# Softmax convolution and a squared-ReLU feed-forward: weight maxima and scaling on GpSimd, scaled chunks from chunk 4, closing sums next to each other

## The chip, the cores and the metric

The kernel runs on one core of one Trainium2 chip. The metric is the device time of one execution in microseconds. The kernel before takes 2104.97 us (median of 3 runs, 2104.33 to 2106.85). The engines are TensorE (PE, its weight loads PEld), VectorE (DVE), ScalarE (ACT), GpSimd (POOL) and SyncE (SP, which only issues transfers).

## The reference

A causal convolution of 7 taps whose weights come from a softmax for each position and head, and then a feed-forward block without a gate, all in float32.

```python
# x (8, 4096, 192), weight_gen (8, 4096, 8, 7), w_in (192, 2048), w_out (2048, 192)
w = weight_gen - np.max(weight_gen, axis=-1, keepdims=True)
w = np.exp(w)
w = w / (np.sum(w, axis=-1, keepdims=True) + 1e-09)
x_pad = np.concatenate([zeros((B, K - 1, D)), x], axis=1)
x_unf = x_pad[:, idx, :].reshape(B, S, K, H, D // H)     # idx: position + tap
x = np.einsum('bshk,bskhg->bshg', w, x_unf).reshape(B * S, D)
h = x @ w_in
r = np.maximum(h, 0.0)
out = (r * r) @ w_out
```

The inputs of the feed-forward weights arrive as float64 and are rounded to float32 in the kernel.

## The kernel before, in words

The 32768 positions are split over 128 partitions with 256 rows each, and worked through in 64 chunks of 4 rows a partition (512 positions). Chunks come in pairs (a group) that share one load of `x` and of the softmax logits. Float32 products are made of parts: each operand is a high part, rounded to the format TensorE takes, and a low part, the rest; high x high, high x low and low x high are added.

A chunk passes through these stages.

- Convolution (`conv_steps`, lines 326 to 500), two chunks ahead. VectorE: maximum (L353), subtraction (L354); ScalarE: exponential (L355); VectorE: sum, reciprocal, product (L356 to L358), then seven products with the taps (L384) and their adds (L397). Some adds are done by a transfer that accumulates (`moved`, L402), issued on GpSimd's queue. Then a transpose (L487) and transfers through DRAM (L493, L498) give `xT`; ScalarE makes the high part `xh` (L427) and VectorE the low part `xl` (L430).
- First product (`mm1`, L522), 8 steps j of a chunk, each 18 matmuls of 64 rows for two of the 16 blocks of the inner dimension.
- ScalarE: ReLU (L539), square (L546), high part (`high`, L550). VectorE: low part (`low`, L559 or L562), one step later.
- Second product (`mm2_turned`), two steps behind the first (LAG). Its 5 x 2 matmuls a block are L638 in an unscaled chunk. In a scaled chunk (`is_scaled`, chunks FIRST = 6 to 62) they are L603, L607 and L613; there the low parts are float16, so the softmax denominators and the weights are multiplied by powers of two that keep them in range, and 32 small matmuls (L613) stand at the end of the chunk in step 1 of the next one.
- Closing (`sum_turned`): ScalarE copies an accumulator (L648), VectorE adds its partner (L650), once for part 0 and once for part 1; only then may TensorE write these accumulators for the next chunk. Part 1 of a scaled chunk is also added across partitions by a transfer on GpSimd's queue (L652). Then transposes (L666, L670), transfers, and the scale of the output taken back (L689).

The weights are decoded during chunk 0 and 1: W holds the high and low parts of `w_in`, V those of `w_out`. For the scaled chunks the kernel needs the largest magnitude of each: `peak_v` (L294) and `peak_w` (L288), four VectorE reductions each in chunks 2 and 3, `spread_peaks` (L302) in chunk 3, step 4, which writes a pair of numbers for each partition to DRAM and reads all of them back on every partition (`dm`, then `tops`, a part of `du`), both on SP, and `coefficients` (L309 to L319) in chunk 3, step 7. `scale_v` multiplies V in place (L323, VectorE) and makes a float16 copy of its high part (L324, ScalarE), eight times, in chunk 5 from step 4 on and chunk 6. `measure` (L270) and `power` (L274 to L277) find a power of two for x, group by group.

Every engine works through its instructions in the order in which they are written. That order is written out by hand: `at(c, j, f)` puts a piece of work into step j of chunk c, `plan_conv` spreads the convolution's steps by a table (two steps of one convolution's end and two of the next one's softmax fall on step 1 of a chunk), and the loop from L878 on walks through the steps. In the step where a scaled chunk closes, the loop does the first two planned pieces (N_AHEAD), then `sum_turned` of part 0, then the other planned pieces, then the high parts, then `sum_turned` of part 1. `stage`, the pool of the tiles called `raw`, has three buffers, used by the weight loads and then by the closing sums.

Of the kernel before, what the change touches and what calls it, by code (L numbers as in the profile page):

```python
# [8 lines left out]
F32 = mybir.dt.float32  # L9
# [13 lines left out]
X_MIN = 2.0 ** -125  # L23
W_MIN = 2.0 ** -80
SHIFT = 2.0 ** 64
G_ROOT = 2.0 ** 8
V_ROOT = 2.0 ** 7
# [3 lines left out]
def kernel(  # L31
# [37 lines left out]
    NBUF = NF // 2  # L69
    FIRST = 6  # L70
    GL_POOL = 5
    SCALE_STEP = NJ
    N_AHEAD = 2
# [50 lines left out]
    scrap = du_flat[:, NF * D // 2 + N:].bitcast(BF16)  # L124
    peaks = const.tile([P, 8], F32, name="peaks")
    tops = du_flat[:, NF * D // 2:NF * D // 2 + 2 * P].bitcast(F32)
# [159 lines left out]

    def peak_w(k):
        nc.vector.tensor_reduce(  # L288
            out=peaks[:, k:k + 1], in_=W[:, 0, 2 * k:2 * k + 2, :].rearrange("p j w -> p (j w)").bitcast(F32),
            axis=AX.X, op=ALU.max, apply_absolute_value=True,  # L290
        )

    def peak_v(k):
        nc.vector.tensor_reduce(  # L294
            out=peaks[:, 4 + k:5 + k], in_=V[:, 4 * k:4 * k + 4, 0:D].bitcast(F32),
            axis=AX.XY, op=ALU.max, apply_absolute_value=True,
        )

    def spread_peaks():
        dm = dram.tile([P, 2], F32, name="dm")  # L300
        pk = coef[:, 4:6]
        nc.vector.tensor_reduce(out=pk, in_=peaks.rearrange("p (w k) -> p w k", w=2), axis=AX.X, op=ALU.max)  # L302
        nc.sync.dma_start(out=dm, in_=pk)
        nc.sync.dma_start(out=tops, in_=dm.rearrange("p w -> (p w)").rearrange("(o n) -> o n", o=1).broadcast_to([P, 2 * P]))

    def coefficients():
# [3 lines left out]
        nc.vector.tensor_scalar_max(top, top, W_MIN)  # L310
        w, v = top[:, 0:1], top[:, 1:2]
        ts(out=w.bitcast(U32), in0=w.bitcast(U32), scalar1=POW2, scalar2=None, op0=ALU.bitwise_and)
        ts(out=w_mul, in0=w, scalar1=SHIFT / G_ROOT, scalar2=None, op0=ALU.mult)
        ts(out=v.bitcast(U32), in0=v.bitcast(U32), scalar1=POW4, scalar2=1, op0=ALU.bitwise_and, op1=ALU.logical_shift_right)
        ts(out=v_unroot, in0=v, scalar1=SHIFT / V_ROOT, scalar2=None, op0=ALU.mult)
# [5 lines left out]
    def scale_v(j):  # L321
        v = V[:, 2 * j:2 * j + 2]
        nc.vector.tensor_scalar(out=v, in0=v.bitcast(F32), scalar1=v_mul, scalar2=None, op0=ALU.mult)  # L323
        nc.scalar.copy(V16[:, 2 * j:2 * j + 2], v[:, :, 0:D].bitcast(F32))  # L324

# [532 lines left out]

    for k in range(4):
        at(2, k + 3, lambda k=k: peak_v(k))  # L860
        at(3, k, lambda k=k: peak_w(k))
    at(3, 4, spread_peaks)
    at(3, 7, coefficients)
    for j in range(NJ):
# [10 lines left out]
    for u in range(1, NU):  # L875
        at(1, 2 * u, lambda u=u: dec(NU + u, 5))

    for c in range(1, NCH):  # L878
        tail = c == NCH - 1
        for j in range(NJ):  # L880
# [28 lines left out]
            if split_sum:  # L909
                for f in fs[:N_AHEAD]:  # L910
                    f()
                del fs[:N_AHEAD]
                sum_turned(done, (0,))
            elif done is not None:
                sum_turned(done)
            for f in fs:
                f()
            if c > 1:
                for part in range(2):
                    if j == (LOAD_STEP if tail else 2 * part + 2 if is_scaled(c - 1) else OUT_STEP + part):  # L920
                        store_turned(c - 1, part)
            if not tail or j < NJ // 2:
                for fb in fbs:
                    high(c, fb)
                    late.append(lambda c=c, fb=fb: low(c, fb))
            if split_sum:
                sum_turned(done, (1,))
            if c == 1 and j == 0:
# [61 lines left out]
```

## Time and profile before

| | |
|---|---|
| median of 3 runs | 2104.97 us |
| the profiled execution's own time | 2101.76 us |
| its span on the core | 2100.0 us |
| TensorE busy | 2074.4 us (99%) |
| VectorE busy | 1870.8 us (89%) |
| ScalarE busy | 1845.2 us (88%) |
| GpSimd busy | 221.2 us (11%) |
| chain that ended last | PE 71%, DVE 15%, DMA 6%, ACT 4% |

The durations in the rows further down come from that one execution. Busy time of TensorE is modelled and does not mean full speed; the weight loads' start times mark the steps more sharply, since 18 loads of L522 begin each step.

### The profile page before, as it was taken

What the parts mean: (1) busy time and instruction counts of PE and PEld (TensorE: products, weight loads), DVE (VectorE), ACT (ScalarE), POOL (GpSimd) and SP (SyncE); (2) the same over time, 40 slices, a digit from 0 to 9 for tenths busy, and PEclk for the clock granted to TensorE, in tenths of its full rate; (3) what the DMA queues carried; (4) which work ended last, traced back from release to release, by engine and by line L of the source; (5) the groups of instructions that cost most, each with busy time, mean ns of one, the idle gap of its engine ahead of it and who ended that gap; (6) DMA issues with size and microseconds to landing.
All of it is one profiled execution on the core that took longest, in us unless ns stands there. A gap on an engine that the chain in (4) does not pass through costs nothing.

```text
span 2100.0 us, 49532 instructions
## 1 busy us (share of the span) xinstructions
PE 2074.4 (99%) x19484; PEld 1707.0 (81%) x19484; DVE 1870.8 (89%) x2953; ACT 1845.2 (88%) x3551; POOL 221.2 (11%) x364
## 2 busy tenths in 40 slices
PE   9999999999999999999999999999999999999999
PEld 8887878878888788888888788787788878888878
DVE  9989899898898898998988988989889889999885
ACT  8887988889888899889898888998888988988986
POOL 0000110111110111101111101111011110011110
PEclk9999999999999999999999999999999999999999
DMA  9524454534545445445355354354453553544522
GB/s 234 101 51 98 108 117 97 122 73 105 125 97 110 93 91 118 113 98 121 70 110 126 94 113 93 90 120 106 104 120 71 110 125 93 116 85 97 122 59 56
DMA packets 322289, 217.78 MB, mean 104 GB/s; under 512 B 215696, under 2 KB 273168, under 8 KB 318216
## 3 DMA queue, kind: packets, MB, share of 16 engines
q1 hardware_dynamic: 300568, 181.17, 37.3%
q0 software_dynamic: 21488, 33.46, 9.4%
q8 instruction: 152, 2.49, 0.5%
q14 instruction: 81, 0.66, 0.1%
HBM read 106.52 MB, written 49.55 MB: 74 GB/s over the span
## 4 chain that ended last, share of the span: by engine, by line
PE 71%; DVE 15%; DMA 6%; ACT 4%; issue 2%; SPq 1%; DVEq 0%; ACTq 0%
PE ph L522 38%; PE acc L603 21%; DMA xT<-xd 4%; PE acc L607 4%; PE acc L613 4%; DVE pr L384 4%; DVE du L559 3%; DVE pr L397 3%; PE acc L638 3%; DVE xl L430 2%; DVE raw L650 1%; DVE gl L559 1%; ACT rg L539 1%; PE acc L570 1%; ACT rg L546 1%
## 5 line engine op out<-in xcount | busy, mean ns | idle before, releaser
L522 PE MATMUL ph<-xh,W 64*128 64x512 f32 x6096 | 1069.0, 403 | 0.0
L522 PEld LDWEIGHTS ph<-xh,W 64*128 64x128 f32 x6096 | 718.3, 186 | 100.9 <-ACT gh L550 23.0
L603 PE MATMUL acc<-gh,V 64*128 64x512 f32 x5472 | 772.9, 378 | 10.1 <-DVE raw L650 8.4
L539 ACT ACTIVATE rg<-ph 128x512 f32<-128x512 f32 x992 | 539.0, 596 | 197.8 <-PE ph L522 193.1
L603 PEld LDWEIGHTS acc<-gh,V 64*128 64x128 f32 x5472 | 594.4, 186 | 104.1 <-DVE raw L650 32.2
L546 ACT ACTIVATE rg<-rg 128x512 f32<-128x512 f32 x1007 | 580.5, 634 | 0.2
L550 ACT CAST gh<-rg 128x512 fp32r<-128x512 f32 x1008 | 576.1, 626 | 3.0 <-PE acc L580 3.0
L522 PE MATMUL ph<-xl,W 64*128 64x512 f32 x3048 | 495.3, 376 | 0.1
L559 DVE TENSOR_TENSOR gl<-rg,gh 128x512 f16<-128x512 f32 x570 | 389.6, 740 | 47.4 <-ACT gh L550 47.4
L384 DVE TENSOR_TENSOR pr<-xt,wt 128x768 f32<-128x768 f32 x440 | 412.3, 949 | 2.3
L522 PEld LDWEIGHTS ph<-xl,W 64*128 64x128 f32 x3048 | 361.5, 186 | 40.4 <-ACT xl L441 0.5
L397 DVE TENSOR_TENSOR pr<-pr 128x768 f32<-128x768 f32 x309 | 295.2, 955 | 6.1
L559 DVE TENSOR_TENSOR du<-rg,gh 128x512 f16<-128x512 f32 x342 | 232.0, 732 | 3.7 <-ACT gh L550 3.7
L607 PE MATMUL acc<-gl,du 64*128 64x512 f16 x1140 | 230.8, 381 | 1.0 <-DVE gl L559 1.0
L430 DVE TENSOR_TENSOR xl<-xT,xh 128x512 fp32r<-128x512 f32 x186 | 122.2, 687 | 122.0 <-ACT xh L427 121.8
L652 POOL DMA_DIRECT2D raw<-raw x57 | 47.3, 830 | 1261.3 <-DVE raw L650 1170.6
L607 PEld LDWEIGHTS <-du 64*128 64x128 f16 x1824 | 101.7, 95 | 62.3 <-issue 4.7
L607 PE MATMUL acc<-du 64*128 64x512 f16 x684 | 138.2, 382 | 0.0
L285 POOL DMA_DIRECT2D x_out<-x_fac x232 | 112.3, 493 | 42.5 <-DVE x_fac L282 41.4
L427 ACT CAST xh<-xT 128x512 fp32r<-128x512 f32 x186 | 108.1, 619 | 9.3 <-DMA xT<-xd 8.6
L402 POOL DMA_DIRECT2D pr<-pr x63 | 57.0, 905 | 531.3 <-DVE pr L384 484.8
L613 PEld LDWEIGHTS <-du 64*64 64x64 f16 x1824 | 48.3, 106 | 57.9 <-issue 24.1
(127 smaller groups left out, 1267.7 us busy)
## 6 DMA issues: line engine op xcount, KB each, us to landing
xT<-xd SPq DMA_DIRECT2D x124, 384.0 KB
xt<-in_x_dram SPq DMA_DIRECT2D x30, 1344.0 KB
out_dram<-o_sb SPq DMA_DIRECT2D x254, 96.0 KB
pr<-pr POOLq DMA_DIRECT2D x63, 384.0 KB, 5.8
xd<-xr SPq DMA_DIRECT2D x248, 96.0 KB
o_sb<-raw SPq DMA_DIRECT2D x342, 64.0 KB
raw<-raw POOLq DMA_DIRECT2D x57, 128.0 KB, 3.9
wt<-in_weight_gen_dram SPq DMA_DIRECT2D x31, 224.0 KB
```

The costliest lines, as they stand in the source:

```text
L285: nc.gpsimd.dma_start(out=fo[b * P // n:(b + 1) * P // n], in_=f[b::n])
L384: tt(out=dst, in0=src, in1=wf[:, t0 * H:t1 * H, k:k + 1].broadcast_to([P, m, G]), op=ALU.mult)
L397: tt(out=prs[k0], in0=prs[k0], in1=prs.pop(k), op=ALU.add)
L430: tt(out=parts["l"][:, k, n], in0=src[k][:, n], in1=parts["h"][:, k, n].bitcast(F32), op=ALU.subtract)
L522: nc.tensor.matmul(two[i], w, order(xx[rows, k]), start=(n == 0), stop=(n == last))
L539: nc.scalar.activation(r, ph, AF.Relu)
L546: nc.scalar.activation(r, r, AF.Square)
L550: nc.scalar.copy(gh, rgs[c, fb])
L559: nc.vector.tensor_tensor(out=gl, in0=g, in1=h, op=ALU.subtract)
L603: nc.tensor.matmul(acc[b + h], V[rows, fb, e:e + P], two_halves(g[rows]), start=fb == 0 and e < 2 * P, stop=False)
L607: nc.tensor.matmul(acc[h], V16[rows, 2 * j + i, 0:P], gls[c, j][rows, i], start=False, stop=last and i == 1)
L613: nc.tensor.matmul(acc[2 + h][i * D1:(i + 1) * D1], V16[rows, 2 * k + i, P:D], gls[c, k][rows, i], start=False, stop=k == NJ - 1, tile_pos ...
```

## The change

The sums of squares of a partition's weights take the place of the largest magnitudes; they are formed on GpSimd (`peaks_of`), folded down to 192 numbers a partition, and VectorE takes the maximum of these. They stand in chunk 1, step 0; the spread follows in chunk 1, step 7, with both transfers on GpSimd's queue, and the coefficients in chunk 2, step 2. V's scaling and its float16 copy are GpSimd's. FIRST is 4. In the closing step both closing sums come before the rest of the planned pieces.

```diff
-W_MIN = 2.0 ** -80
+W_MIN = 2.0 ** -123
-G_ROOT = 2.0 ** 8
+G_ROOT = 2.0 ** 9
...
-    FIRST = 6
+    FIRST = 4
     GL_POOL = 5
+    PEAKS = 192
...
-    def peak_w(k):
-        nc.vector.tensor_reduce(
-            out=peaks[:, k:k + 1], in_=W[:, 0, 2 * k:2 * k + 2, :].rearrange("p j w -> p (j w)").bitcast(F32),
-            axis=AX.X, op=ALU.max, apply_absolute_value=True,
-        )
-
-    def peak_v(k):
...
+    def peaks_of(pieces, k):
+        tt = nc.gpsimd.tensor_tensor
+        both = stage.tile([P, 2, NF * D // 4], F32, name="raw")
+        for i, w in enumerate(pieces):
+            o = both[:, min(i, 1)]
+            shaped = o if len(w.shape) == 2 else o.rearrange("p (a b) -> p a b", b=D)
+            tt(out=shaped, in0=w, in1=w, op=ALU.mult)
+            if i:
+                tt(out=both[:, 0], in0=both[:, 0], in1=o, op=ALU.add)
+        n, v = both.shape[2], both[:, 0]
+        while n > PEAKS:
+            n //= 2
+            tt(out=v[:, 0:n], in0=v[:, 0:n], in1=v[:, n:2 * n], op=ALU.add)
+        peaks[k] = v[:, 0:n]
 
     def spread_peaks():
         dm = dram.tile([P, 2], F32, name="dm")
         pk = coef[:, 4:6]
-        nc.vector.tensor_reduce(out=pk, in_=peaks.rearrange("p (w k) -> p w k", w=2), axis=AX.X, op=ALU.max)
-        nc.sync.dma_start(out=dm, in_=pk)
-        nc.sync.dma_start(out=tops, in_=dm.rearrange("p w -> (p w)").rearrange("(o n) -> o n", o=1).broadcast_to([P, 2 * P]))
+        for k in range(2):
+            nc.vector.tensor_reduce(out=pk[:, k:k + 1], in_=peaks[k], axis=AX.X, op=ALU.max)
+        nc.gpsimd.dma_start(out=dm, in_=pk)
+        nc.gpsimd.dma_start(out=tops, in_=dm.rearrange("p w -> (p w)").rearrange("(o n) -> o n", o=1).broadcast_to([P, 2 * P]))
 
     def coefficients():
...
-        w, v = top[:, 0:1], top[:, 1:2]
-        ts(out=w.bitcast(U32), in0=w.bitcast(U32), scalar1=POW2, scalar2=None, op0=ALU.bitwise_and)
+        tu = top.bitcast(U32)
+        ts(out=tu, in0=tu, scalar1=POW4, scalar2=1, op0=ALU.bitwise_and, op1=ALU.logical_shift_right)
+        ts(out=top, in0=top, scalar1=SHIFT, scalar2=None, op0=ALU.mult)
+        w, v, vu = top[:, 0:1], top[:, 1:2], tu[:, 1:2]
...
     def scale_v(j):
         v = V[:, 2 * j:2 * j + 2]
-        nc.vector.tensor_scalar(out=v, in0=v.bitcast(F32), scalar1=v_mul, scalar2=None, op0=ALU.mult)
-        nc.scalar.copy(V16[:, 2 * j:2 * j + 2], v[:, :, 0:D].bitcast(F32))
+        nc.gpsimd.tensor_scalar(out=v, in0=v.bitcast(F32), scalar1=v_mul, scalar2=None, op0=ALU.mult)
+        nc.gpsimd.tensor_copy(V16[:, 2 * j:2 * j + 2], v[:, :, 0:D].bitcast(F32))
...
-    for k in range(4):
-        at(2, k + 3, lambda k=k: peak_v(k))
-        at(3, k, lambda k=k: peak_w(k))
-    at(3, 4, spread_peaks)
-    at(3, 7, coefficients)
+    at(1, 0, lambda: peaks_of([W[:, 0, 2 * k:2 * k + 2].rearrange("p j w -> p (j w)").bitcast(F32) for k in range(4)], 0))
+    at(1, 0, lambda: peaks_of([V[:, 4 * k:4 * k + 4, 0:D].bitcast(F32) for k in range(4)], 1))
+    at(1, 7, spread_peaks)
+    at(2, 2, coefficients)
...
+    def highs_of(c, fbs):
+        for fb in fbs:
+            high(c, fb)
+            late.append(lambda fb=fb: low(c, fb))
...
+            if split_sum:
+                highs_of(c, fbs)
+                sum_turned(done, (1,))
             for f in fs:
                 f()
...
-            if not tail or j < NJ // 2:
-                for fb in fbs:
-                    high(c, fb)
-                    late.append(lambda c=c, fb=fb: low(c, fb))
-            if split_sum:
-                sum_turned(done, (1,))
+            if not split_sum and (not tail or j < NJ // 2):
+                highs_of(c, fbs)
```

Line numbers of the changed kernel are some 7 higher where the functions are the same. The first place is GpSimd's queue in chunk 1. Before, the accumulating transfers stand one behind the other; the third of the first row is chunk 2's tap 3, `pr<-prw` is its tap 4, and what follows belongs to chunks 3 to 5.

```order
L159 MEMSET xt 128x1152
L402 DMA pr<-pr 128x768
L402 DMA prx<-pr 128x768
L402 DMA pr<-pr 128x768 x3
L402 DMA pr<-prw 128x768
L402 DMA pr<-pr 128x768 x2
L402 DMA pr<-prw 128x768
L402 DMA pr<-pr 128x768 x2
```

In the changed kernel this is the end of the second sum of squares (on V) and what follows it on the same queue; the first sum, of the same make, stands ahead, directly behind the row `pr<-pr 128x768 x3`.

```order
L294 TENSOR_TENSOR raw<-V 128x768
L296 TENSOR_TENSOR raw<-raw 128x768
L300 TENSOR_TENSOR raw<-raw 128x384
L300 TENSOR_TENSOR raw<-raw 128x192
L409 DMA pr<-prw 128x768
L409 DMA pr<-pr 128x768 x2
L308 DMA dm<-coef 128x2
L309 DMA du<-dm 128x256
L409 DMA pr<-prw 128x768
L409 DMA pr<-pr 128x768
```

Chunk 2's tap 4 (the first `pr<-prw`) moved behind 18 GpSimd instructions, and chunk 3's (the second) behind the two transfers of the spread.

The second place is VectorE in the closing step of a scaled chunk, here chunk 23 closing in chunk 24 (the steps of the other scaled chunks read alike). Before:

```order
L384 TENSOR_TENSOR pr<-xt,wt 128x768
L397 TENSOR_TENSOR pr<-pr 128x768
L650 TENSOR_TENSOR raw<-acc_12036,raw 128x512
L353 TENSOR_REDUCE mx<-wt 128x32
L354 TENSOR_TENSOR wt<-wt,mx 128x224
L650 TENSOR_TENSOR raw<-acc_12038,raw 128x512
L559 TENSOR_TENSOR gl<-rg,gh 128x2x256 x2
```

And in the changed kernel:

```order
L391 TENSOR_TENSOR pr<-xt,wt 128x768
L404 TENSOR_TENSOR pr<-pr 128x768
L657 TENSOR_TENSOR raw<-acc_12008,raw 128x512
L657 TENSOR_TENSOR raw<-acc_12010,raw 128x512
L360 TENSOR_REDUCE mx<-wt 128x32
L361 TENSOR_TENSOR wt<-wt,mx 128x224
L566 TENSOR_TENSOR gl<-rg,gh 128x2x256 x2
```

The second closing sum moved ahead of the maximum and the subtraction; nothing else changed places.

The third place is VectorE from the spread to the coefficients, in chunks 1 and 2 of the changed kernel.

```order
L307 TENSOR_REDUCE coef<-raw 128x1 x2
L391 TENSOR_TENSOR prw<-xt,wt 128x768
L391 TENSOR_TENSOR pr<-xt,wt 128x768
L569 TENSOR_TENSOR gl<-rg,gh 128x512 x2
L391 TENSOR_TENSOR pr<-xt,wt 128x768
L404 TENSOR_TENSOR pr<-pr 128x768
L569 TENSOR_TENSOR gl<-rg,gh 128x512 x2
L657 TENSOR_TENSOR raw<-acc_826,raw 128x512
L657 TENSOR_TENSOR raw<-acc_824,raw 128x512
L404 TENSOR_TENSOR pr<-pr 128x768 x2
L360 TENSOR_REDUCE mx<-wt 128x32
L361 TENSOR_TENSOR wt<-wt,mx 128x224
```

Behind these rows stand two low parts and then the read of the maxima (`coef<-du`), which before stood in chunk 3, behind the low parts of its step 6.

## Rows read from the trace of the kernel before

**Rows 1.** The page, part 1: busy time of each engine.

```profile
PE 2074.4 (99%) x19484; PEld 1707.0 (81%) x19484; DVE 1870.8 (89%) x2953; ACT 1845.2 (88%) x3551; POOL 221.2 (11%) x364
```

**Rows 2.** Busy times by stretch: start:end, length, then busy time of each engine.

```profile
core 0: us, PE busy (x) PEld busy (x) DVE busy (x) ACT busy (x) POOL busy (x), PEclk, DMA share, GB/s
290.02:2025.58 1735.56, 1727.82 (x16419) 1406.39 (x16418) 1562.41 (x2431) 1545.00 (x2971) 197.51 (x323) 1.00 0.47 103
```

**Rows 3.** In order of time (start, length, what): weight loads, chunk 62.

```profile
2025.58 0.83 PEld L522 LDWEIGHTS ph<-xh,W 64*128 64x128 f32 x6
...
2035.32 0.51 PEld L522 LDWEIGHTS ph<-xh,W 64*128 64x128 f32 x6 [0.41 <-ACT gh L550]
...
2057.31 0.62 PEld L522 LDWEIGHTS ph<-xh,W 64*128 64x128 f32 x6
```

**Rows 4.** In order of time: ScalarE's copy and VectorE, chunk 29 closing.

```profile
1007.14 0.59 ACT L648 COPY raw<-acc 128x512 f32<-128x512 f32 x1 [0.16 <-PE acc L613]
...
1007.82 0.68 DVE L650 TENSOR_TENSOR raw<-acc,raw 128x512 f32<-128x512 f32 x1
...
1008.42 0.37 DVE L353 TENSOR_REDUCE mx<-wt 128x32 f32<-128x224 f32 x1
...
1008.83 0.39 DVE L354 TENSOR_TENSOR wt<-wt,mx 128x224 f32<-128x224 f32 x1
...
1009.14 0.68 DVE L650 TENSOR_TENSOR raw<-acc,raw 128x512 f32<-128x512 f32 x1
```

**Rows 5.** In order of time: weight loads of the same step.

```profile
1009.88 0.73 PEld L603 LDWEIGHTS acc<-gh,V 64*128 64x128 f32 x7 [0.39 <-DVE raw L650]
```

**Rows 6.** In order of time: SP, VectorE and TensorE around the coefficients, chunk 4.

```profile
137.63 12.19 SPq L680 DMA_DIRECT2D o_sb<-raw  x16
...
156.93 0.42 DVE L309 TENSOR_REDUCE coef<-du 128x2 f32<-128x256 f32 x1 [9.04 <-DMA du<-dm]
...
162.21 0.80 PE L638 MATMUL acc<-gl,V 64*128 64x512 f32 x2 [8.45 <-DVE gl L562]
```

**Rows 7.** Busy times by stretch: after TensorE's gap (columns as in rows 2).

```profile
162.20:166.20 4.00, 3.99 (x24) 3.32 (x26) 4.00 (x6) 0.92 (x2) 0.00 (x0) 0.64 0.94 334
```

**Rows 8.** In order of time: first weight loads of chunks 5, 6 and 8.

```profile
190.06 0.62 PEld L522 LDWEIGHTS ph<-xh,W 64*128 64x128 f32 x6
...
222.86 0.62 PEld L522 LDWEIGHTS ph<-xh,W 64*128 64x128 f32 x6
...
290.02 0.83 PEld L522 LDWEIGHTS ph<-xh,W 64*128 64x128 f32 x6
```

**Rows 9.** In order of time: VectorE and TensorE in chunk 1.

```profile
66.85 1.94 DVE L397 TENSOR_TENSOR pr<-pr 128x768 f32<-128x768 f32 x2
...
70.59 1.22 DVE L562 TENSOR_TENSOR gl<-rg,gh 128x512 fp32r<-128x512 f32 x2
...
70.56 0.59 PE L638 MATMUL acc<-gh,V 64*128 64x512 f32 x2
71.27 0.48 PE L638 MATMUL acc<-gl,V 64*128 64x512 f32 x2
```

**Rows 10.** Line L430 from 290 to 2030 us: VectorE's idle time before it.

```profile
  ACT xh L427: 113.9, 54
```

**Rows 11.** Groups by line: VectorE's maxima of W.

```profile
L288 DVE TENSOR_REDUCE peaks<-W 128x1 f32<-128x768 f32 x4 | 3.8, 943 | 0.0
```

**Rows 12.** In order of time: GpSimd in chunk 1.

```profile
57.72 0.86 POOL L402 DMA_DIRECT2D pr<-pr  x1 [1.11 <-issue]
60.19 0.86 POOL L402 DMA_DIRECT2D pr<-prw  x1 [1.62 <-DVE wt L354]
```

**Rows 13.** Groups by line (busy us, mean ns): GpSimd before 40 us.

```profile
L159 POOL MEMSET xt<- 128x1152 f32 x1 | 1.1, 1062 | 0.0
...
masks.py:199 POOL TENSOR_SCALAR_AFFINE_SELECT ident<-ident 128x128 f32<-128x128 f32 x1 | 0.3, 289 | 0.1
masks.py:197 POOL MEMSET ident<- 128x128 f32 x1 | 0.2, 205 | 0.0
```

**Rows 14.** Transfers by tile: KB each, median us from issue to landing.

```profile
pr<-prw POOLq DMA_DIRECT2D x2, 384.0 KB, 4.1
```

**Rows 15.** Busy times by stretch: chunk 1 (columns as in rows 2).

```profile
58.00:68.00 10.00, 10.00 (x96) 8.76 (x96) 9.11 (x15) 10.00 (x22) 1.43 (x2) 1.00 0.56 101
```

More of the change, by code (lines that the diff above doesn't have):

```diff
@@ L124 @@
     scrap = du_flat[:, NF * D // 2 + N:].bitcast(BF16)
-    peaks = const.tile([P, 8], F32, name="peaks")
+    peaks = {}
     tops = du_flat[:, NF * D // 2:NF * D // 2 + 2 * P].bitcast(F32)
@@ L285, in factor @@
             nc.gpsimd.dma_start(out=fo[b * P // n:(b + 1) * P // n], in_=f[b::n])
-    def peak_w(k):
-        nc.vector.tensor_reduce(
-            out=peaks[:, k:k + 1], in_=W[:, 0, 2 * k:2 * k + 2, :].rearrange("p j w -> p (j w)").bitcast(F32),
-            axis=AX.X, op=ALU.max, apply_absolute_value=True,
-        )
-    def peak_v(k):
[L294 to L297, printed above, removed]
+    def peaks_of(pieces, k):
[12 more added lines that the diff above has]
+        peaks[k] = v[:, 0:n]
     def spread_peaks():
@@ L310, in coefficients @@
         nc.vector.tensor_scalar_max(top, top, W_MIN)
-        w, v = top[:, 0:1], top[:, 1:2]
-        ts(out=w.bitcast(U32), in0=w.bitcast(U32), scalar1=POW2, scalar2=None, op0=ALU.bitwise_and)
+        tu = top.bitcast(U32)
+        ts(out=tu, in0=tu, scalar1=POW4, scalar2=1, op0=ALU.bitwise_and, op1=ALU.logical_shift_right)
+        ts(out=top, in0=top, scalar1=SHIFT, scalar2=None, op0=ALU.mult)
+        w, v, vu = top[:, 0:1], top[:, 1:2], tu[:, 1:2]
         ts(out=w_mul, in0=w, scalar1=SHIFT / G_ROOT, scalar2=None, op0=ALU.mult)
-        ts(out=v.bitcast(U32), in0=v.bitcast(U32), scalar1=POW4, scalar2=1, op0=ALU.bitwise_and, op1=ALU.logical_shift_right)
+        ts(out=vu, in0=vu, scalar1=POW4, scalar2=1, op0=ALU.bitwise_and, op1=ALU.logical_shift_right)
         ts(out=v_unroot, in0=v, scalar1=SHIFT / V_ROOT, scalar2=None, op0=ALU.mult)
```

## The prediction

> **What bounds the kernel now.** I read the page first. TensorE is busy for 99% of the span [rows 1], so time is gained or lost only where TensorE waits or takes more steps; the other engines count where TensorE waits for them. Then the busy times by stretch and the weight loads in order of time, which give the length of a chunk. From the 9th chunk (chunk 8, counted from 0) to the start of chunk 62, 54 chunks take 1735.56 us, 32.14 each [rows 2]. Chunk 62, whose step 1 carries no softmax steps, runs from 2025.58 to 2057.31, 31.73 us [rows 3]: the same matmuls without the wait. So a scaled chunk waits 0.41 us on average, 22.1 us over the 54.
>
> Where it waits is in the step after a chunk's last matmuls. As chunk 29 closes, ScalarE has copied the second accumulator by 1007.73, but VectorE runs first sum (1007.82), maximum (1008.42), subtraction (1008.83), and only then the second sum (1009.14, done 1009.82) [rows 4]. TensorE's weight loads for the next accumulation stop until 1009.88 [rows 5]. A load that stands idle is partly covered by matmuls still running, which is why I use chunk lengths, not these idle times.
>
> Three other places matter, all early. In chunk 4 VectorE waits 9.04 us for the broadcast maxima [rows 6], since the transfer that begins it stands on SP behind 16 stores from 137.63 to 149.82; the two transfers themselves end at 156.9, 7.1 us later. [...] Second, chunks 4 and 5 are unscaled; chunk 5 takes 32.80 us, from 190.06 to 222.86, and I count as much for chunk 4 without its wait. The first two scaled ones, chunks 6 and 7, take 67.16 together, to 290.02 [rows 8]. Third, in chunk 1 TensorE has no slack towards VectorE: its matmuls on a low part start at 71.27, 0.71 us after those before them at 70.56, on a low part begun at 70.59 [rows 9].
>
> **The change part by part.**
>
> *Closing sums.* With maximum and subtraction moved behind, the second sum starts about 0.62 us after the first (1008.42 less 1007.82 plus a hand-over), so it ends 0.7 us earlier, at about 1009.1 [rows 4], before the weights for that accumulator are wanted. Of the 22.1 us I keep 21: in a few chunks VectorE is so late that even the first sum comes too late, about 1 us in all. The softmax start is 0.7 us later, and the exponential runs in the step behind; VectorE waits 113.9 us in 54 places, 2.1 us a chunk, for ScalarE's high parts [rows 10], so there is room. Gain 21 us.
>
> *Coefficients.* The spread is now in chunk 1 and its two transfers are on GpSimd's queue. From there to the coefficients VectorE has some 11 us of other work; the transfers took 7.1. The wait goes: 8.45 + 1.4 = 9.9 us gained. The eight reductions (0.943 us for each of four on W [rows 11], and as many on V) go too, but stand beside a TensorE that had enough work; I count nothing for them. No wait stands behind them that would come out.
>
> *Two more scaled chunks.* If the scaled stretch begins without a wait, chunk 4 is two unscaled steps of 4.10 (32.80 / 8) and six scaled ones of 21.99 together (2035.32 to 2057.31 [rows 3]), 30.2, and chunks 5 to 7 take 31.73 each: 125.4 against 2 x 32.80 + 67.16 = 132.8, a gain of 7.4. If the first two scaled chunks wait as they do now (67.16 - 30.2 - 31.7 = 5.3), 2.1 is left. I take 4, since part of what they wait for, the copies on ScalarE and the scaling on VectorE, leaves these engines.
>
> *Sums of squares on GpSimd.* This is the loss. Eighteen instructions, 14 on 768 elements a partition, two on 384 and two on 192, stand in GpSimd's queue between the transfer issued at 57.72 and the one at 60.19 [rows 12]; that one, which adds tap 4 of chunk 2 to its sum, now waits for all eighteen. VectorE needs its result for the last add of chunk 2's convolution (the second of the two from 66.85 on, at 67.8 [rows 9]) and stands still in its queue until then; behind it are the transpose and the low part that TensorE has no slack for. The trace has no GpSimd instruction with two inputs. A one-input one took 289 ns for 128 elements, a memset 205 for 128 and 1062 for 1152 [rows 13]: the memset costs 0.84 ns an element on 0.10 us, and a read 0.66 ns more. One write and two reads come to 2.15 ns an element, 1.74 us for 768, 0.92 for 384, 0.51 for 192: 14 x 1.74 + 2 x 1.43 = 27.2 us. Bounds: the memset's rate (0.74 us, 11.7 in all) from below; a quarter more than my rate, 34 us, from above. With 27.2 the chain ends at 58.6 + 27.2 = 85.8, the transfer lands 4.1 us later [rows 14] at 89.9, and VectorE waits 22.1 us. TensorE waits as long, and pays the 1.4 us of clock seen in chunk 4: a loss of 23.5 us, from 8 to 30.
>
> [...]
>
> *Scaling and float16 copy on GpSimd.* Eight pairs, one to a step of about 4 us; at 1.50 ns an element a pair takes some 1.9 us, and the scaled weights are wanted six steps later. Nothing waits, if GpSimd does not hold up VectorE. *Coefficients, measuring and x's power two chunks earlier, and the move of chunk 3's tap 4 behind the spread's transfers:* 2.5 us of VectorE work in a chunk where low parts are a few tenths to 2 us ahead. I take 1.5, from 0 to 5.
>
> **Sum** against the profiled execution's own 2101.76: -21 - 9.9 - 4 + 23.5 + 1.5 = -9.9, 2091.9. The median of the runs is 2104.97, 3.2 above the profiled one; the forecast in those terms is 2095.
>
> **Rivals.**
>
> *VectorE and GpSimd hold each other up.* Then the eighteen run between VectorE's two-input instructions. VectorE is busy 9.11 of the 10 us from 58 on [rows 15], some 8.3 of it with two SBUF inputs, which end GpSimd's chain that much later; while it scales, GpSimd holds VectorE up by perhaps 1.5 of 1.9 us a step where VectorE has about 0.4 idle (1562.41 busy of 1735.56 [rows 2]), 9 at most in eight steps, 5 taken. 2095 + 8.3 + 5 = 2108, from 2102 to 2113. For it: VectorE is full and nearly all its instructions there have two inputs. Against it: no row; GpSimd does no arithmetic beside VectorE in this trace. It decides for slower once the mutual waiting is over 10 us. [...]
>
> *GpSimd is quick.* At the memset's rate the chain is over 15.5 us earlier: 2095 - 15.5 = 2080.
>
> *The closing sums give nothing back.* If VectorE, not the order of its instructions, set the chunk's length, the 0.41 us a chunk would return at the next low part: 2095 + 21 = 2116, slower. It decides where VectorE's idle time a chunk is under 0.41 us; it is 2.1 at one wait alone [rows 10], and chunk 62 ran freely with less VectorE work, so it is unlikely.
>
> **How the numbers follow.** The forecast 0.44 (its own range 2086 to 2102), mutual waiting 0.32, quick GpSimd 0.10, nothing from the closing sums 0.08, mixtures 0.06. What can be told from no change is about 0.2%, 4.2 us. Faster: 0.38 of the forecast (its upper end is within 4.2 us), 0.04 + 0.10 + 0.01 of the others, 0.53. Same: 0.06 + 0.17 + 0.02 = 0.25. Slower: 0.11 + 0.08 + 0.03 = 0.22. The range 2083 to 2112 takes in most of mutual waiting and leaves out the quick GpSimd and the last rival.
>
> **What would show it.** Closing sums: the two sums adjacent on VectorE, the weight loads of that step unbroken, chunks of 31.7 to 31.8 us. Coefficients: no wait of VectorE for the broadcast. Sums of squares: the eighteen on GpSimd at 1.74 us for 768 elements, the next transfer issued near 86, one VectorE wait of some 22 us at the last add of chunk 2, and a gap of TensorE as long in chunk 1 with a low clock behind it. Mutual waiting would show as longer VectorE adds or gaps between them beside GpSimd's, and a chain of 35 us. The prediction is wrong if TensorE shows no gap in chunk 1, or if the steady chunk stays at 32.1.

## The result, and the profile after

The changed kernel takes 2118.88 us (median of 4 runs, 2116.29 to 2122.32), the one before beside it 2104.65; the ratio is 1.0069, 95% interval 1.0051 to 1.0087. It is 0.7% slower, where I had forecast 2095 and a range up to 2112. Its profiled execution took 2119.23 us, the span 17.4 us more than before's 2100.0.

Lines of code stand 7 further down than before (L522 is L529, L562 is L569, L650 is L657). The page of the changed kernel, part 1 (compare [rows 1]):

```profile
span 2117.4 us, 49553 instructions
...
PE 2070.6 (98%) x19484; PEld 1693.2 (80%) x19484; DVE 1882.0 (89%) x2941; ACT 1837.1 (87%) x3545; POOL 289.2 (14%) x412
```

TensorE does the same work and is busy for less of a longer span. Where the span grew is read from the first weight load of each chunk:

| chunks | before, us | after, us | difference |
|---|---|---|---|
| 0 | 38.68 | 39.56 | +0.9 |
| 1 | 29.39 | 57.44 | +28.0 |
| 2 and 3 | 65.81 | 65.92 | +0.1 |
| 4 to 7 | 142.91 | 131.22 | -11.7 |
| 8 to 61 | 1735.56 | 1735.95 | +0.4 |

Chunk 1 is the loss. In order of time (start, length, what), GpSimd in chunk 1 of the changed kernel, answering to [rows 12]:

```profile
59.26 3.21 POOL L294 TENSOR_TENSOR raw<-W 128x768 f32<-128x768 f32 x2
62.55 2.41 POOL L296 TENSOR_TENSOR raw<-raw 128x768 f32<-128x768 f32 x1
...
86.17 1.47 POOL L294 TENSOR_TENSOR raw<-V 128x768 f32<-128x768 f32 x1
87.71 1.81 POOL L296 TENSOR_TENSOR raw<-raw 128x768 f32<-128x768 f32 x1
...
91.20 0.87 POOL L409 DMA_DIRECT2D pr<-prw  x1
```

The eighteen run from 59.26 to 91.2, 32 us, and the transfer of tap 4 leaves behind them, 31 us later than before. VectorE in the kernel before, where GpSimd has no such work:

```profile
58.31 0.95 DVE L384 TENSOR_TENSOR prw<-xt,wt 128x768 f32<-128x768 f32 x1
59.18 0.38 DVE L353 TENSOR_REDUCE mx<-wt 128x32 f32<-128x224 f32 x1
...
61.98 1.82 DVE L384 TENSOR_TENSOR pr<-xt,wt 128x768 f32<-128x768 f32 x2
```

And VectorE in the changed kernel:

```profile
59.29 4.00 DVE L391 TENSOR_TENSOR prw<-xt,wt 128x768 f32<-128x768 f32 x1
63.22 0.37 DVE L360 TENSOR_REDUCE mx<-wt 128x32 f32<-128x224 f32 x1
63.62 1.58 DVE L361 TENSOR_TENSOR wt<-wt,mx 128x224 f32<-128x224 f32 x1
65.13 4.17 DVE L569 TENSOR_TENSOR gl<-rg,gh 128x512 fp32r<-128x512 f32 x2
...
82.21 2.22 DVE L404 TENSOR_TENSOR pr<-pr 128x768 f32<-128x768 f32 x1
95.23 0.96 DVE L404 TENSOR_TENSOR pr<-pr 128x768 f32<-128x768 f32 x1 [10.81 <-DMA pr<-prw]
```

Two things are to be seen. The last add waits 10.81 us for the transfer, as forecast in kind. But the work ahead of it, from the multiplication at 59.29 to the end of the add at 84.4, takes 25.1 us; the same instructions took 9.5 before (58.31 to 67.8 [rows 9]). A multiplication takes 4.00 us instead of 0.95, the subtraction 1.58 instead of 0.39 [rows 4], while the maximum, with one input, keeps its time (0.37, 0.38 before). GpSimd's instructions are longer too: 2.41 us beside VectorE at 62.55, 1.81 for the same one at 87.71, where VectorE stands still. So 15.6 us of stretching and 10.8 of waiting reach TensorE, whose longest wait there is for a low part:

```profile
98.68 0.29 PEld L645 LDWEIGHTS acc<-gl,V 64*128 64x128 f32 x2 [12.38 <-DVE gl L569]
```

In the 3.30 us behind this wait the granted clock averages 0.56 (columns as in [rows 2]): the trace has it at 0.50 of full speed from 98.7 to 100.7 us and at 1.00 from 101.7 to 103.7. By an estimate, 3.30 x 0.44, that costs 1.5 us more:

```profile
98.70:102.00 3.30, 3.30 (x18) 2.68 (x20) 3.27 (x7) 0.00 (x0) 0.00 (x0) 0.56 0.42 86
```

Stretching, waiting and clock come to 27.9 us, near the 28.0 of the table. The wait for the broadcast maxima [rows 6] is gone; VectorE reads them in chunk 2 without idle time before it:

```profile
124.26 0.41 DVE L314 TENSOR_REDUCE coef<-du 128x2 f32<-128x256 f32 x1
```

The 54 steady chunks, chunks 8 to 61, did not move: 32.15 us each, which the prediction names as a sign that it is wrong. Busy times by stretch, as in [rows 2]:

```profile
307.28:2043.23 1735.95, 1721.32 (x16419) 1400.63 (x16418) 1560.97 (x2431) 1539.01 (x2971) 197.13 (x323) 1.00 0.47 103
```

That average hides two kinds of chunk. In order of time, a chunk in which the closing came as I forecast, from the stores of the transposed x (L500) and the loads of xT (L505) in chunk 20 to the closing in chunk 21:

```profile
707.85 1.81 SPq L500 DMA_DIRECT2D xd<-xr  x4
711.54 1.29 SPq L505 DMA_DIRECT2D xT<-xd  x2
...
717.76 0.62 ACT L434 CAST xh<-xT 128x512 fp32r<-128x512 f32 x1
...
734.86 1.28 DVE L657 TENSOR_TENSOR raw<-acc,raw 128x512 f32<-128x512 f32 x2
```

And two chunks later, from the transposition in chunk 22 on:

```profile
769.84 0.98 DVE L494 STREAM_TRANSPOSE xr<-pr 128x768 f32<-128x768 f32 x1
...
770.85 1.84 SPq L500 DMA_DIRECT2D xd<-xr  x4
776.10 1.29 SPq L505 DMA_DIRECT2D xT<-xd  x2
...
783.39 0.62 ACT L434 CAST xh<-xT 128x512 fp32r<-128x512 f32 x1 [2.37 <-DMA xT<-xd]
...
784.04 0.69 DVE L437 TENSOR_TENSOR xl<-xT,xh 128x512 fp32r<-128x512 f32 x1 [3.54 <-ACT xh L434]
...
800.50 1.28 DVE L657 TENSOR_TENSOR raw<-acc,raw 128x512 f32<-128x512 f32 x2
...
801.24 0.30 PEld L610 LDWEIGHTS acc<-gh,V 64*128 64x128 f32 x4 [1.88 <-DVE raw L657]
```

Both sums stand together in both (x2 in one row), so the edit does what it says. But in the second case the loads of xT leave 5.25 us behind the stores instead of 3.7, the high part starts 12.6 us behind the transposition's end instead of 9.9, VectorE waits 3.54 us for it, and the first sum comes 3.2 us into TensorE's step instead of 0.8. The chunk that follows, 23, takes 33.45 us, chunk 21 took 31.73. From the start of the low part to the end of the next transposition it is 20.6 to 20.8 us in every steady chunk of both kernels. So there is a loop beside TensorE's own pace: transposition, two transfers through DRAM, ScalarE's copy, VectorE's low part, 20.7 us of VectorE, transposition. A round of it is 31.2 to 33.8 us long after the change and 31.9 to 32.9 before; TensorE's shortest chunk is 31.52. The 2.1 us a chunk of [rows 10], which I took for room, is where this loop passes from the transfers to VectorE.

### The profile page after: what moved, and what is told of

Read it like the earlier page. It is cut to its first block, busy times and chain, and to the rows that moved or that the text cites. A ratio compares the mean times of both kernels' runs of the same rounds, so it can differ in the third digit from the quotient of the medians.

```text
span 2117.4 us, 49553 instructions
## 1 busy us (share of the span) xinstructions
PE 2070.6 (98%) x19484; PEld 1693.2 (80%) x19484; DVE 1882.0 (89%) x2941; ACT 1837.1 (87%) x3545; POOL 289.2 (14%) x412
## 4 chain that ended last, share of the span: by engine, by line
PE 67%; DVE 15%; DMA 6%; ACT 5%; issue 2%; POOL 1%; SPq 1%; DVEq 0%; ACTq 0%; POOLq 0%
PE ph L529 35%; PE acc L610 21%; DMA xT<-xd 6%; PE acc L614 5%; DVE pr L391 4%; PE acc L620 4%; DVE du L566 3%; DVE pr L404 3%; DVE xl L437 2%; PE acc L645 2%; ACT rg L546 1%; ACT gh L557 1%; DVE gl L566 1%; ACT rg L553 1%; ACT du L271 1%
## 5 line engine op out<-in xcount | busy, mean ns | idle before, releaser
L529 PE MATMUL ph<-xh,W 64*128 64x512 f32 x6096 | 1014.0, 404 | 0.0
L610 PE MATMUL acc<-gh,V 64*128 64x512 f32 x5664 | 761.9, 378 | 17.1 <-DVE raw L657 16.7
L529 PEld LDWEIGHTS ph<-xh,W 64*128 64x128 f32 x6096 | 674.7, 186 | 104.9 <-ACT gh L557 18.9
L529 PE MATMUL ph<-xl,W 64*128 64x512 f32 x3048 | 466.3, 376 | 0.1
L566 DVE TENSOR_TENSOR gl<-rg,gh 128x512 f16<-128x512 f32 x590 | 405.7, 744 | 22.0 <-ACT gh L557 21.6
L529 PEld LDWEIGHTS ph<-xl,W 64*128 64x128 f32 x3048 | 339.6, 186 | 36.2 <-ACT xl L448 0.5
L404 DVE TENSOR_TENSOR pr<-pr 128x768 f32<-128x768 f32 x307 | 296.0, 964 | 17.1 <-DMA pr<-prw 10.8
L566 DVE TENSOR_TENSOR du<-rg,gh 128x512 f16<-128x512 f32 x354 | 240.4, 733 | 3.7 <-ACT gh L557 3.7
L614 PE MATMUL acc<-gl,du 64*128 64x512 f16 x1180 | 216.9, 381 | 0.7 <-DVE gl L566 0.7
L614 PEld LDWEIGHTS <-du 64*128 64x128 f16 x1888 | 89.8, 95 | 81.1 <-issue 41.7
L614 PE MATMUL acc<-du 64*128 64x512 f16 x708 | 130.1, 382 | 0.0
```

The costliest lines, as they stand in the source:

```text
L404: tt(out=prs[k0], in0=prs[k0], in1=prs.pop(k), op=ALU.add)
L529: nc.tensor.matmul(two[i], w, order(xx[rows, k]), start=(n == 0), stop=(n == last))
L566: nc.vector.tensor_tensor(out=gl, in0=g, in1=h, op=ALU.subtract)
L610: nc.tensor.matmul(acc[b + h], V[rows, fb, e:e + P], two_halves(g[rows]), start=fb == 0 and e < 2 * P, stop=False)
L614: nc.tensor.matmul(acc[h], V16[rows, 2 * j + i, 0:P], gls[c, j][rows, i], start=False, stop=last and i == 1)
```

## The experiments

Each was compared with runs of the kernel before on the same chip; lengths of chunks are from its profile.

**e1 and e2: the closing sums alone, and all but the closing sums.** e1 is the kernel before with

```
+            if split_sum:
+                highs_of(c, fbs)
+                sum_turned(done, (1,))
             for f in fs:
...
-            if split_sum:
-                sum_turned(done, (1,))
```

and e2 the changed kernel with these lines taken back.

> The kernel before with only the closing sums moved ahead of the softmax steps. Loop theory (a steady chunk is set by the way from VectorE's transposition over the two transfers through DRAM, ScalarE's copy of the high part and VectorE's subtraction back to the next transposition, some 10 to 11 us of transfers and 20.7 us of VectorE without idle time): both sums come in time, but VectorE is no earlier at the next transposition, so the 54 chunks stay near 32.1 us; gain 0 to 10 us, 2095 to 2105. Rival 'real but given back' (the sums gain the 21 us that I forecast, and another part of the change spoils the steady chunks): 2084, chunks of 31.75. Rival 'the new order is itself harmful': over 2108.

> The changed kernel with the second closing sum put back behind the softmax steps and the high parts; all else as changed. Loop theory: the same time as the changed kernel within 5 us, 2114 to 2124. Rival 'real but given back': if the early parts of the change spoil the steady chunks by themselves, undoing the sums loses a further 21 us, about 2140.

e1: 2089.24 us, ratio 0.9942 (0.9930 to 0.9954). e2: 2124.35 us, ratio 1.0106 (1.0089 to 1.0122). The 54 chunks of e1, then of e2:

```profile
290.34:2014.14 1723.80, 1719.93 (x16420) 1393.82 (x16418) 1560.56 (x2431) 1540.83 (x2971) 197.75 (x323) 1.00 0.48 104
```

```profile
305.65:2049.49 1743.84, 1731.01 (x16420) 1406.83 (x16418) 1563.98 (x2431) 1544.02 (x2971) 197.70 (x323) 1.00 0.47 102
```

Neither theory had it whole. The sums are worth 11.8 us in the steady chunks on their own and 7.9 in the changed kernel, not 21 and not nothing. And the early parts, which touch no line of a steady chunk, cost 8.3 us there (e2 against [rows 2]). Four edits that I had priced one by one were not independent.

**e3: GpSimd's chain behind the transfer that it held up.**

```
-    at(1, 0, lambda: peaks_of(...))
...
-    at(1, 7, spread_peaks)
-    at(2, 2, coefficients)
+    at(2, 3, coefficients)
...
+    at(1, 1, lambda: peaks_of(...))
...
+    at(2, 0, spread_peaks)
```

Both calls of `peaks_of` stand behind `plan_conv` of chunks 2 and 3 here.

> The changed kernel with the 18 sums of squares queued on GpSimd behind the transfer of chunk 2's tap 4 instead of ahead of it (spread and coefficients one step later with them). Theory 'place in the queue': the stall of 28 us in chunk 1 falls to about 6 (now chunk 3's three transfers stand behind the chain), some 2097. Rival 'mutual hold-up': VectorE's longer instructions beside GpSimd's are what TensorE waits for, and 18 us or more of the stall stay, 2109 or more.

2109.62 us, ratio 1.0037 (1.0025 to 1.0049); chunk 1 takes 49.58 us, still 20.2 more than before. GpSimd and VectorE in chunk 1 of e3, in order of time:

```profile
60.88 0.86 POOL L409 DMA_DIRECT2D pr<-prw  x1 [1.61 <-DVE wt L361]
61.44 3.22 POOL L294 TENSOR_TENSOR raw<-W 128x768 f32<-128x768 f32 x2
...
61.46 5.98 DVE L569 TENSOR_TENSOR gl<-rg,gh 128x512 fp32r<-128x512 f32 x2 [0.79 <-ACT gh L557]
67.36 4.70 DVE L391 TENSOR_TENSOR pr<-xt,wt 128x768 f32<-128x768 f32 x2
72.10 2.10 DVE L404 TENSOR_TENSOR pr<-pr 128x768 f32<-128x768 f32 x1
74.12 3.42 DVE L241 TENSOR_TENSOR V<-du,V 128x512 fp32r<-128x512 f32 x2
...
95.51 1.28 DVE L569 TENSOR_TENSOR gl<-rg,gh 128x512 fp32r<-128x512 f32 x2
```

The transfer leaves first and VectorE never waits from 62 to 97 us, yet up to the chain's end at 94.7 most rows with two inputs take twice their usual time or more (4.70 for two multiplications that take 1.82 before). Behind it the two low parts are back at 1.28 us. The place in the queue was worth 8 us; the hold-up of two engines is the rest. My condition for the rival (2109 or more) is met.

**e4: the first split of x one step later** in the changed kernel, which takes the transfers out of the loop.

```
-                at(m - 1, NJ - 3 if k == 0 and is_scaled(m) else NJ - 2, f)
+                at(m - 1, NJ - 2, f)
```

> The changed kernel with the first split of a scaled chunk's x (ScalarE's high part, VectorE's low part) one step later, in the step of the second. VectorE's work is the same; only its wait for the transfers is taken out of the loop. Loop theory: steady chunks of 31.55 to 31.75 us, 54 x 0.5 = 27 us less, about 2092. Rival 'VectorE's work alone sets the length': chunks stay at 32.15, 2119 within 4. Rival 'given back by the early parts': no change either.

2102.89 us, ratio to before 1.0004 (0.9996 to 1.0013). The 54 chunks:

```profile
308.55:2029.59 1721.04, 1721.04 (x16420) 1404.14 (x16418) 1562.66 (x2432) 1540.75 (x2971) 197.69 (x323) 1.00 0.47 104
```

31.87 us each, and every chunk alike within 0.02. The loop theory's sign is right, since VectorE's work is the same 1562 us; its size is not (14.9 us of the 27 expected): VectorE, now later in its order, starts the first sum 1.4 us into the step in every chunk.

**e5 and e6: where TensorE's code stands.** What spoils some chunks repeats with a period of 8. So do the packets of TensorE's code, the transfers that bring its instructions; the transfer queues of the changed kernel (packets, MB, share):

```profile
q8 instruction: 152, 2.49, 0.5%
```

152 packets of 16 KB for 38,968 instructions of TensorE is one for 256.4. TensorE starts 4864 of them in 8 scaled chunks, and 19 packets begin there (114 in chunks 8 to 55, before and after), one for 256; that the packets are TensorE's code is my inference from these counts. By it they come at the same places every 8 chunks, and, by an estimate, moved by 32 instructions they hit the same places in other chunks (3 chunks are 1824 instructions, 7 x 256 and 32). After the change chunk 8 stands 9 instructions later in this code: between 186.6 and 214.0, in chunks 4 to 6, TensorE has nine semaphore instructions that it does not have before. I moved the code by tiny matmuls at the very start, 12 in the changed kernel (e5), 4 in the kernel before (e6):

```
+    for _ in range(12):
+        nc.tensor.matmul(awake[:, 0:16], ident, ident[:, 0:16], start=True, stop=True)
```

> The changed kernel with twelve tiny matmuls (16 columns, result unused) ahead of everything, so that TensorE's instructions stand 24 places later in its code. In the traces TensorE's code comes in packets of 16 KB, 19 of them in 8 chunks (4864 instructions), and one that begins within about 3 us behind the transposition ends the stores to DRAM 1 to 1.5 us late. The change moved TensorE's place in this rhythm by 9 instructions; with 24 more it stands as before (33, of a pattern that repeats every 32). Code-load theory: the 54 steady chunks fall from 1736 to some 1725, as with the closing sums alone, and the time from 2119 to some 2109. Rival 'another effect of the early parts' (GpSimd's transfers, the buffers' rotation): steady chunks stay within 3 us of 1736, 2119 to 2121.

> The mirror image: the kernel before with four tiny matmuls ahead of everything, 8 instructions, which puts TensorE's code where the changed kernel has it (9). Code-load theory: the 54 steady chunks rise from 1735.6 to some 1743, as in the changed kernel with the old sums, worst in the chunks of number 1, 2 and 7 modulo 8 instead of 4 and 5, and the time to some 2110. Rival 'another effect of the early parts': steady chunks within 3 us of 1735.6, worst in 4 and 5, 2102.

The expectations count two instructions for each tiny matmul. The pages, e5's and then e6's, show four, two matmuls and two weight loads (19484 of each without them):

```profile
PE 2070.5 (98%) x19508; PEld 1667.0 (79%) x19508; DVE 1881.6 (89%) x2941; ACT 1838.3 (87%) x3545; POOL 289.4 (14%) x412
```

```profile
PE 2079.6 (99%) x19492; PEld 1710.2 (81%) x19492; DVE 1871.5 (89%) x2953; ACT 1842.8 (87%) x3551; POOL 220.8 (10%) x364
```

So the code moved by 48 and 16 instructions, not by 24 and 8. Counted from the kernel before and in a repeat of 32, e6 stands at 16 where the changed kernel has 9, and e5 at 25 (9 + 48 - 32) where I meant it to stand at 1.

e5: 2109.41 us, ratio 1.0026 (1.0017 to 1.0035). e6: 2115.95 us, ratio 1.0056 (1.0044 to 1.0069). The 54 chunks of e5, then of e6:

```profile
309.10:2033.38 1724.28, 1717.37 (x16419) 1367.44 (x16418) 1560.17 (x2430) 1539.89 (x2970) 197.15 (x323) 1.00 0.47 104
```

```profile
290.88:2035.62 1744.74, 1729.94 (x16419) 1406.13 (x16417) 1563.14 (x2431) 1542.71 (x2971) 197.16 (x323) 1.00 0.47 102
```

One moved 11.7 us down, the other 9.2 us up; 1725 and 1743 were expected. As neither stood where it was meant to, it is partly luck that the sizes fit so well. What the two show is that unused instructions ahead of everything move the steady chunks by this much, in e6 with none of the early parts there. Mean length of the chunks 8 to 61 by number modulo 8:

```
              0      1      2      3      4      5      6      7
before      31.98  32.05  32.19  32.08  32.42  32.40  31.98  31.98
e6          31.98  32.69  32.15  32.18  32.01  32.02  31.98  33.59
e2          31.98  32.90  32.44  32.31  31.99  31.99  31.98  32.77
after       31.77  32.69  32.15  32.22  31.83  31.64  31.60  33.38
e5          31.73  31.62  31.62  32.18  32.18  31.73  31.71  32.77
```

Sixteen unused instructions give the kernel before nearly the pattern of the changed one, longest in 1 and 7. The 48 do not give back that of before: in e5 the chunks of number 7 stay the longest. The transfers' records show how the packets act.

Over before, after, e1, e2, e5, e6 and e11 (chunks 8 to 60, 371 in all), a code packet begins within 3.2 us behind the transposition in 100 chunks; the stores to DRAM then end 4.05 us behind it (median) and in 84 of the 100 later than 3.6. In the other 271 they end at 3.13, and 10 are later than 3.6.

A second place shows in the same records. Where no packet begins within 3.2 us but one does 5.5 to 8.3 us behind the transposition (30 chunks; the bounds are read off these rows), the stores end on time, at 3.16, but the high part, which waits for the loads of xT, starts at 11.59 us (median), in 25 of the 30 at 11 or later. In the 241 chunks with a packet in neither place it starts at 10.62, in 21 at 11 or later. The long chunks of number 1 in "after" and e6 follow such packets, those of number 7 the packets at the stores.

How late the high part starts gives the next chunk's length:

```
high part behind the transposition, us   chunks   next chunk, us
under 10                                    26        31.73
10 to 11                                   254        31.90
11 to 11.5                                  50        32.45
11.5 to 12                                  17        32.83
over 12                                     24        33.48
```

**e7 and e8: the kernel before with the late split and the spread's two transfers on GpSimd's queue**, with (e7) and without (e8) the closing sums' move.

> The kernel before (maxima on VectorE, scaled from chunk 6 on) with three edits: the closing sums moved ahead, the spread's two transfers on GpSimd's queue, and the first split of a scaled chunk one step later. Loop theory with what the runs gave: chunks of 31.87 as with the changed kernel's late split, 14.5 us less, and VectorE's wait for the maxima gone, 10 us less: about 2077. If the late split helped only because of the early parts' rhythm: chunks of 31.92 or more, 2080 to 2090.

> The same without the closing sums' move: the kernel before with the late split and the two transfers on GpSimd's queue. It shows what the closing sums are worth once the transposition is no longer late. If the sums' place is a bound of its own, as I forecast: chunks of 32.1 and 12 us or more slower than with the move, about 2090. If the loop alone set the chunks: the same as with the move within 4 us, about 2077.

e7: 2082.83 us, ratio 0.9899 (0.9885 to 0.9912). e8: 2120.71 us, ratio 1.0084 (1.0070 to 1.0098). Their 54 chunks, e7 first:

```profile
285.48:2006.17 1720.69, 1720.69 (x16420) 1403.56 (x16419) 1561.98 (x2432) 1540.60 (x2971) 196.81 (x323) 1.00 0.47 104
```

```profile
283.41:2043.19 1759.78, 1727.94 (x16420) 1403.52 (x16418) 1565.55 (x2432) 1543.23 (x2971) 196.82 (x323) 1.00 0.47 101
```

VectorE in chunk 18 of e8, where chunk 17 closes, in order of time:

```profile
620.40 0.68 DVE L650 TENSOR_TENSOR raw<-acc,raw 128x512 f32<-128x512 f32 x1
621.00 0.37 DVE L353 TENSOR_REDUCE mx<-wt 128x32 f32<-128x224 f32 x1
621.41 0.39 DVE L354 TENSOR_TENSOR wt<-wt,mx 128x224 f32<-128x224 f32 x1
621.72 0.68 DVE L650 TENSOR_TENSOR raw<-acc,raw 128x512 f32<-128x512 f32 x1
```

With the transfers out of the loop every chunk of either kernel is alike, and the sums' place is worth 39.1 us, where I expected 12 or more: 0.72 a chunk, as much as the maximum and the subtraction between the two sums take there (621.00 to 621.72). This is the mechanism that I had forecast, free of the loop. The late split without the sums' move makes the kernel slower, the sums alone gain 12.8 us; together, with the queue, they gain 21.

**e9 and e12: what the wait for the maxima had covered.** The steady chunks of e7 came out as expected, its time 6 us over the 2077, and its chunk 4 still takes 39.81 us. e9 puts the coefficients later; e12 also puts chunk 3's load of x earlier.

```
-    at(3, 7, coefficients)
+    at(4, 2, coefficients)
...
-            if j == (LOAD_STEP if c > 1 else 0) and c % 2 ...
+            if j == (2 if c == 3 else LOAD_STEP if c > 1 else 0) and c % 2 ...
```

> The kernel before with late split, closing sums ahead, the spread's transfers on GpSimd's queue, and now the coefficients three steps later (chunk 4, step 2). In the run without this last edit chunk 4 still took 39.8 us, because the second transfer stood behind its first on GpSimd until 143.8 and VectorE came for its result too early. If VectorE's wait for the maxima is all that chunk 4 loses: chunk 4 falls to about 33, 7 us less, 2076. Rival: the chunk waits for something else there as well (the kernel before with its wait took 42.9, one with the late split alone 36.6), and 3 us or more stay, 2079 or more.

> The run with the later coefficients, and in chunk 3 alone the load of the next x group three steps earlier, ahead of that chunk's 28 stores on SP instead of behind them. In the run before it ScalarE's measuring waited 6.2 us in chunk 4 for that load (and VectorE 3.5 us), which VectorE's wait for the maxima had covered in the kernel before. If that is what is left of chunk 4's loss: chunk 4 from 39.2 to some 33, 2077. Rival: a third wait stands behind it, or the early load takes the transfers' time from chunk 3: 2081 or more.

e9: 2083.31 us, ratio 0.9907 (0.9893 to 0.9920); chunk 4 still 39.16 us, so the rival's condition (2079 or more) is met. ScalarE in chunk 4 of e9:

```profile
167.03 1.48 ACT L270 ACTIVATE du<-xt 128x1536 bf16<-128x1536 f32 x1 [6.24 <-DMA xt<-in_x_dram]
```

In the kernel before ScalarE came to this instruction at 169.82 without a wait: VectorE's 9.04 us [rows 6] had covered it. e12: 2079.27 us, ratio 0.9892 (0.9876 to 0.9909), chunk 4 at 32.81 us, what an unscaled chunk takes [rows 8]. Of the 6.4 us the profiled run of e12 gave 2.2 back by a later start of chunk 0 (15.4 us against 13.2), which I can't explain; that start lies between 13.1 and 13.8 in the other profiles, but for e5's with its matmuls ahead (16.1). e12 beats both kernels.

**e10: both low parts another step later.**

```
-        splits = [split(k) for k in range(ND)]
+        splits = [lambda k=k: high_part(k) for k in range(ND)] + [lambda k=k: low_part(k) for k in range(ND)]
...
+                at(m - 1, NJ - 2 if k < ND else NJ - 1, f)
```

> The same, with both low parts of a scaled chunk's x another step later, behind both high parts: VectorE no longer waits 2.1 us a chunk for ScalarE's high part. If that wait is what makes the first closing sum 0.6 us late in every chunk (it starts 1.38 us into the step, its input is there at 0.69): chunks of 31.55 to 31.73, 8 to 16 us less than with the low parts in place. Rival 'the high part's place in ScalarE's order sets it, or the low parts come too late for the next chunk's first matmuls': no gain, or a loss of several us.

2132.97 us, ratio 1.0144 (1.0128 to 1.0159). A miss: step 2 falls to 3.58 us as hoped, but step 0 rises from 3.68 to 4.88, because the low parts come too late for the next chunk's first matmuls; 32.72 us a chunk.

**e11: w_out's scaling back on VectorE and ScalarE** in the changed kernel.

```
-        nc.gpsimd.tensor_scalar(out=v, ...)
-        nc.gpsimd.tensor_copy(V16[...], ...)
+        nc.vector.tensor_scalar(out=v, ...)
+        nc.scalar.copy(V16[...], ...)
```

> The changed kernel with w_out's scaling back on VectorE and its float16 copy back on ScalarE; all else as changed. Mutual hold-up: GpSimd's scaling of 2.2 to 3.7 us a pair stretches VectorE's low parts beside it from 1.28 to 1.9 us, in chunks 3 to 5; without it those chunks lose 1 to 4 us less, 2115 to 2118. Rival 'GpSimd takes the work off VectorE at no cost': VectorE has 0.8 us more a step and the chunks are 1 to 4 us longer, 2120 to 2123.

2106.47 us, ratio 1.0016 (1.0007 to 1.0025), 12 us under the changed kernel. Chunks 3 to 5 fell by 0.8 us, so the hold-up there is small. The gain is in the steady chunks, 1725.25 us, which this edit does not touch: a high part over 12 us behind the transposition comes in 2 chunks instead of 7. TensorE's code stands at the same place here, with the nine semaphore instructions. In chunk 30 the packet begins at 3.1 us behind the transposition and does no harm, where in the changed kernel it began at 2.8 and did. In the chunks of number 0 modulo 8 it begins 5.6 to 7.8 us behind the transposition in the changed kernel, and the next chunk takes 32.4 to 33.0 us; here it begins at 8.4 or later in five of seven, and 31.52 follows; in the other two it begins at 7.2 and 8.3, and 32.53 and 33.35 follow. That fits the code packets; what moved them against the transposition was not tried.

## Why the prediction was wrong

- **Closing sums, -21: the step that failed**, where the prediction says "Of the 22.1 us I keep 21". It took the first sum's time as given and only moved the second. The runs show that the first sum comes at the end of the loop over DRAM; where the high part is late, what the move spares TensorE is lost again. In the changed kernel's surroundings the move is worth 7.9 us (e2), alone 11.8 (e1), free of the loop 39.1 (e7, e8). The supporting reading, "so there is room", was wrong: the 2.1 us were a wait in that loop.
- **A missing term, +8.3.** The early parts slow the steady chunks (e2), and moving TensorE's code alone does so too (e6, 9.2 us by 16 instructions); the long chunks are those where a code packet falls on the stores or loads. The nine instructions of the change are not enough by themselves: e11 has them, and its steady chunks are only 1.5 us longer than e1's (1725.25, 1723.80). What else moves the packets against the transposition stays open. No term and no rival had any of this.
- **Sums of squares, +23.5: right in kind, 28.0 measured.** A 768-element instruction at 1.47 to 1.81 us where VectorE stands still is what I estimated (1.74). But the queue's wait was 10.8 us instead of 22.1, and 15.6 came from stretched VectorE instructions; the clock's 1.5 was right (1.4). e3 shows that mending the queue alone saves 8. The rival that had this mechanism gave it 13 us; alone it costs 20.
- **Coefficients, -9.9: right, 10.1** (chunk 4's 42.94 us against 32.81 for an unscaled one). The 8.45 is TensorE's wait in [rows 6]; no run shows the 1.4 by itself, it is an estimate from [rows 7], 4.00 us at a mean clock of 0.64 (4.00 x 0.36). In chunk 4 of the changed kernel the granted clock is 1.00. That nothing stands behind the wait was wrong for a kernel scaled from chunk 6 on (e9); the changed kernel escapes most of it (ScalarE waits 2.8 us for that load).
- **Two more scaled chunks, -4: 1.6** (132.8 us without the wait against 131.2). A pair of scaling and copy on GpSimd took 3.7 us on average instead of 1.9; e11 puts what that held up at 0.8 us.
- **The rest, +1.5: 0.1** in chunks 2 and 3, where it was expected. Chunk 0 is 0.9 longer, which no term covers; it lies between 38.67 and 40.94 us in the profiles.

The measured terms sum to -7.9 + 8.3 + 28.0 - 10.1 - 1.6 + 0.1 + 0.9 = 17.7, the span's difference is 17.4. The rival "the closing sums give nothing back" comes near in time (2116) but not in cause: VectorE's work does not set the chunk, since e4 and e7 shorten it with the same work.

## What to carry over

When an engine idles in every round and the same stretch of work follows each time, the idle time need not be room; follow it back to its own start, and if that closes a loop, compare the loop's length with the bound engine's. Price edits of one loop together, and after a wait is taken away look at what was waiting beside it. Here a GpSimd chain of two-input instructions next to a full VectorE cost VectorE's time (15.6 us of stretching in chunk 1), not only its own queue's (10.8).

## What I had not expected of the hardware

- Where a 16 KB packet of TensorE's code fell among the small stores to DRAM, they ended 0.9 us late (median 4.05 against 3.13 us, 100 and 271 chunks); where one fell on the loads behind them, the high part was about 1 us late (11.59 against 10.62, 30 and 241 chunks). Sixteen unused instructions at the start cost 9.2 us in 54 chunks of one kernel, 48 gained 11.7 in the other.
- Beside GpSimd's two-input instructions VectorE's with two inputs took as much as four times as long (0.95 to 4.00 us), a reduction with one did not (0.38 and 0.37), and GpSimd's took a third more (1.81 to 2.41).
